# A convolution's taps move from VectorE to GpSimd, in a kernel of two chained MLPs

## The chip, the cores and the metric

One NeuronCore of a Trainium2 chip. The metric is the device time of one execution in microseconds, lower is better. Engines by the names of the profile: PE is TensorE's matmul, PEld its weight load, DVE is VectorE, ACT is ScalarE, POOL is GpSimd, SP is SyncE, which issues nearly all of the DMAs.

## The reference

A causal convolution over 7 positions whose taps are a softmax of `weight` (one set for each of 8 heads, 24 channels a head), and two MLPs behind it, all in float32. 8192 tokens (2 x 4096), 192 channels, hidden width 2048.

```python
w = exp(weight - max); w = w / (sum(w) + 1e-9)          # (8, 7)
out = einsum('hk,bskhg->bshg', w, x_unf)                # 7 taps for each channel
h = x @ w_in                                            # first MLP
g = where(h >= 1, h, where(h <= -1, 0, (h + 1)**2 / 4))
x = g @ w_out
h = x @ w_in2                                           # second MLP
g = h * (1 / (1 + exp(-1.702 * h)))
return g @ w_out2
```

## The kernel before

Tokens lie along the free dimension, channels on the partitions. The 8192 tokens are 16 blocks of T = 512. The 192 channels of a block are a tile of 128 (part 0, `xa`) and one of 64; the 64 last channels of two blocks that follow each other share one tile of 128 partitions (part 1, `xb`). So block pair j has three convolutions of seven taps over 128x512: part 0 of block 2j, the joint part 1, and part 0 of block 2j+1. A convolved tile is split into two float32r tiles, a high half copied by ACT and the rest subtracted by DVE (`split`, L72); the same is done with the hidden values and the weights, and a product is made of three such pairs.

The hidden width is cut into NF = 16 slices. A unit is one slice of one phase; a phase is one MLP of one block. The order of units is fixed (`units`, L219): blocks 0 and 1 of the first MLP in turn, four slices of each at a time (units 0 to 31), then block 2 (units 32 to 47), then the second MLP of blocks 0 and 1, and so on. One step of the first loop (L493, steps 0 to 47) makes `gemm1` of its unit (five matmuls into a PSUM bank `h`), its activation (`act_a`: ACT L272 and L273, DVE L274), the split of the unit before (`act_b`: ACT L73, DVE L74), `gemm2` of the unit four steps back (five matmuls into `acc`), and then what is planned beside it. From step 48 on two units go together (`both`).

What goes beside a step stands in `plan`: `at(step, op)` appends to a list, and `beside(step)` issues that list. The order within an engine is the order of issue; an engine waits only for data and buffers. Beside the first steps the weights are converted: `convert_at(1, f, ...)` loads slice f three steps ahead (`raw`, three buffers) and works on it in four steps, s to s+3, with s = f-2 for slices 4 to 7 and 2f-9 from slice 8 on: `begin` (ACT L117, DVE L118), `join` (DVE L122), `high_part` (ACT L127), `low_part` (DVE L131, L132). So the low part of slice 11 is issued at step 16 and wanted by unit 19, that of slice 15 at step 24 and wanted by unit 27.

The convolutions of blocks 0 and 1 are made ahead of the loop, on DVE and, with diagonal matrices `diag` (L165), on PE; POOL scales one set of these matrices (L167, seven multiplications of 128x128). All others are planned by `conv_at(j)`, L424, on DVE (`conv_taps`, L148: a multiplication L152, then six fused multiply-adds L153). For j = 1 the first unit of block 2 is 32 and that of block 3 is 80: its inputs are loaded at step 2, seven taps into `cva` stand at steps 10 to 16, `put_a` (the split) at 17, seven taps into `cvb` at 18 to 24, `put_b` at 25, and the taps of block 3's part 0 at 65 to 71.

The tag `o` (two buffers, pool `o_p`) holds the diagonals first and the outputs later. `xt` has two buffers for part 0 and one for part 1.

Of the kernel before, what the change touches and what calls it, by code (L numbers as in the profile page):

```python
# [8 lines left out]
F32 = mybir.dt.float32  # L9
# [6 lines left out]
P = 128  # L16
T = 512
# [3 lines left out]
def kernel(  # L21
# [21 lines left out]
    nc = tc.nc  # L43
    NBLK, D, _ = out.shape
    K = taps_in.shape[2]
    NF, _, WC = w1.shape
    DB = D - P
    B = P // DB
# [14 lines left out]
    o_p = ctx.enter_context(tc.tile_pool(name="o", bufs=2))  # L63
    ps = ctx.enter_context(tc.tile_pool(name="ps", bufs=1, space=bass.MemoryType.PSUM))

    def bank(n, name):
        return ps.tile([P, T], F32, tag=f"bank{n}", name=name)
# [4 lines left out]
    def split(src, hi, lo):  # L72
        nc.scalar.copy(hi, src)  # L73
        nc.vector.tensor_sub(lo, src, f32(hi))  # L74


    taps = const.tile([P, 2, K], F32, name="taps")
# [61 lines left out]
    def new_xs():  # L139
        return [xs_p.tile([P, T], F32R, tag=t, name=t) for t in ("xah", "xal", "xb", "xc")]  # L140

    def x_load(part, i):

        t = xt_p.tile([P, T + 64], F32, tag=f"xt{part}", name="xt", bufs=2 - part)[:, 0 : PAD + T]
        nc.sync.dma_start(t, (xb if part else xa)[i])
        return t

    def conv_taps(part, t, c):  # L148
        def tap(k):
            w, x = taps[:, part, k : k + 1], t[:, k : k + T]  # L150
            if k == 0:
                return lambda: nc.vector.tensor_scalar_mul(c, x, w)  # L152
            return lambda: nc.vector.scalar_tensor_tensor(c, x, w, c, op0=ALU.mult, op1=ALU.add)  # L153

        return [tap(k) for k in range(K)]

    def warm_up():

        w = bank(7, "warm")
        for _ in range(9):  # L160
            nc.tensor.matmul(w[:, 0:P], ident, ident, start=True, stop=True)
# [12 lines left out]
    def put_a(i, c):  # L174
        split(c, *x1[i][:2])

    def swap_halves(dst, src):
        nc.sync.dma_start(f32(dst[0:DB]), f32(src[DB:P]))
        nc.sync.dma_start(f32(dst[DB:P]), f32(src[0:DB]))

    def put_b(i, c):

        b, halved = i % B, phases.index((1, i)) * NF >= WHOLE
        t = x1[i][2 + (b if halved else 0)]
        hi, lo = (t[0:DB], t[DB:P]) if b == 0 else (t[DB:P], t[0:DB])
        split(c[b * DB : (b + 1) * DB], hi, lo)
        if halved:
            swap_halves(x1[i][3 - b], t)

    def conv_ops(j):  # L190

        ta, tb = xt[0, B * j], xt[1, j]
        ca = cv_p.tile([P, T], F32, tag="cva", name="cva")
        cb = cv_p.tile([P, T], F32, tag="cvb", name="cvb", bufs=1)
        x1[B * j] = new_xs()
        ops = conv_taps(0, ta, ca) + [lambda: put_a(B * j, ca)]
        ops += conv_taps(1, tb, cb) + [lambda: put_b(B * j, cb)]
        st = {}

        def begin():  # L200
            st["c"] = cv_p.tile([P, T], F32, tag="cva", name="cva")
            x1[B * j + 1] = new_xs()
            st["ops"] = conv_taps(0, xt[0, B * j + 1], st["c"])
            put_b(B * j + 1, cb)

        ops.append(begin)
        ops += [lambda: st["ops"].pop(0)() for _ in range(K)] + [lambda: put_a(B * j + 1, st["c"])]
        return ops
# [195 lines left out]
    def at(step, op):  # L404
        plan.setdefault(max(step, 0), []).append(op)
# [14 lines left out]
    def fetch_x(*which):  # L420
        for part, i in which:
            xt[part, i] = x_load(part, i)

    def conv_at(j):  # L424
        first, second = (unit_at[phases.index((1, B * j + k)), 0] for k in range(B))
        ops = []
        at(first - 30, lambda: fetch_x((0, B * j), (1, j), (0, B * j + 1)))
        at(first - 22, lambda: ops.extend(conv_ops(j)))
        for k in range(2 * (K + 1)):
            at(first - 22 + k, lambda: ops.pop(0)())  # L430
        for k in range(K + 2):
            at(second - 16 + k, lambda: ops.pop(0)())

    with tc.manual_schedule():
        nc.sync.dma_start(taps, taps_in)
# [5 lines left out]

        make_identity(nc, ident)
        warm_up()
        softmax_taps()

# [3 lines left out]
        ca = cv_p.tile([P, T], F32, tag="cva", name="cva")  # L449
# [31 lines left out]
        for j in range(1, NBLK // B):  # L481
            conv_at(j)
# [97 lines left out]
```

## Time and profile before

| | us |
|---|---|
| median of 3 runs | 1138.7 (1138.65 to 1138.96) |
| the profiled execution | 1138.51 |
| its span, first to last instruction | 1136.7 |
| PE busy | 1127.7 (99%) |
| ACT busy | 823.0 (72%) |
| DVE busy | 713.6 (63%) |
| POOL busy | 6.7 (1%, 13 instructions) |

A busy time is the sum over an engine's instructions; those of PE overlap, so a busy PE need not be PE at its peak. The shares are those of the whole span; the first 80 us have other shares than the rest. Times in rows count from the span's start. "idle before <- releaser" is the time in which an engine stood ahead of an instruction, and what ended that time.

### The profile page before, as it was taken

What the parts mean: (1) busy time and instruction counts of PE and PEld (TensorE: products, weight loads), DVE (VectorE), ACT (ScalarE), POOL (GpSimd) and SP (SyncE); (2) the same over time, 40 slices, a digit from 0 to 9 for tenths busy, and PEclk for the clock granted to TensorE, in tenths of its full rate; (3) what the DMA queues carried; (4) which work ended last, traced back from release to release, by engine and by line L of the source; (5) the groups of instructions that cost most, each with busy time, mean ns of one, the idle gap of its engine ahead of it and who ended that gap; (6) DMA issues with size and microseconds to landing.
All of it is one profiled execution on the core that took longest, in us unless ns stands there. A gap on an engine that the chain in (4) does not pass through costs nothing.

```text
span 1136.7 us, 22822 instructions
## 1 busy us (share of the span) xinstructions
PE 1127.7 (99%) x9324; PEld 927.1 (82%) x9324; DVE 713.6 (63%) x1152; ACT 823.0 (72%) x1468; POOL 6.7 (1%) x13
## 2 busy tenths in 40 slices
PE   9999999999999999999999999999999999999998
PEld 5878888888888888888888888888888888888886
DVE  7998765675557756476564756647566575655532
ACT  7989875867758677686776768677586776868654
POOL 2000000000000000000000000000000000000000
PEclk9999999999999999999999999999999999999999
DMA  5321420100001000010000100010000100000000
GB/s 176 124 65 43 123 76 11 57 10 25 10 11 43 17 18 10 11 43 20 15 19 12 33 20 15 20 43 1 20 15 20 44 1 20 15 20 15 11 15 14
DMA packets 16680, 36.40 MB, mean 32 GB/s; under 512 B 2497, under 2 KB 2753, under 8 KB 16577
## 3 DMA queue, kind: packets, MB, share of 16 engines
q1 hardware_dynamic: 16432, 34.82, 10.4%
q8 instruction: 73, 1.20, 0.5%
q14 instruction: 31, 0.25, 0.1%
q10 hardware_dynamic: 144, 0.13, 0.0%
HBM read 21.05 MB, written 6.29 MB: 24 GB/s over the span
## 4 chain that ended last, share of the span: by engine, by line
PE 94%; DVE 3%; ACT 2%; issue 1%; DMA 0%; SPq 0%
PE acc L361 46%; PE h L361 42%; PE acc L315 3%; PE h L250 3%; DVE glo L74 1%; DVE a L274 1%; PE ca_ps L170 1%; DVE wd L122 0%; DVE cva L153 0%; DMA raw<-in_w_dram 0%; ACT a L273 0%; ACT a L272 0%; ACT wa L117 0%; ACT wt L127 0%; DVE wt L131 0%
## 5 line engine op out<-in xcount | busy, mean ns | idle before, releaser
L361 PE MATMUL acc<-ghi,wt 64*128 64x512 f32 x2772 | 835.1, 386 | 0.0
L361 PE MATMUL h<-xah,wt 64*128 64x512 f32 x1848 | 713.6, 386 | 0.0
L361 PE MATMUL acc<-glo,wt 64*128 64x512 f32 x1848 | 678.0, 386 | 0.0
L361 PEld LDWEIGHTS acc<-ghi,wt 64*128 64x128 f32 x2772 | 468.5, 184 | 53.9 <-ACT ghi L73 0.3
L74 DVE TENSOR_TENSOR glo<-a,ghi 128x512 fp32r<-128x512 f32 x512 | 341.3, 688 | 232.9 <-ACT ghi L73 223.6
L361 PEld LDWEIGHTS acc<-glo,wt 64*128 64x128 f32 x1848 | 340.0, 184 | 36.5 <-DVE glo L74 0.8
L361 PEld LDWEIGHTS h<-xah,wt 64*128 64x128 f32 x1848 | 340.0, 184 | 36.2 <-issue 0.4
L361 PE MATMUL h<-xal,wt 64*128 64x512 f32 x924 | 356.8, 386 | 0.0
L73 ACT CAST ghi<-a 128x512 fp32r<-128x512 f32 x512 | 301.3, 614 | 26.2 <-DVE a L274 25.7
L274 DVE SCALAR_TENSOR_TENSOR a<-h,a 128x512 f32<-128x512 f32 x256 | 176.8, 690 | 159.7 <-ACT a L273 159.4
L276 ACT ACTIVATE a<-h 128x512 f32<-128x512 f32 x256 | 150.8, 596 | 153.9 <-PE h L361 146.0
L361 PE MATMUL h<-xb,wt 64*128 64x512 f32 x693 | 230.9, 386 | 0.0
L361 PE MATMUL h<-xc,wt 64*128 64x512 f32 x693 | 230.7, 386 | 0.0
L272 ACT ACTIVATE a<-h 128x512 f32<-128x512 f32 x256 | 151.0, 590 | 53.0 <-PE h L361 52.3
L361 PEld LDWEIGHTS h<-xal,wt 64*128 64x128 f32 x924 | 170.0, 184 | 17.9
L273 ACT ACTIVATE a<-a 128x512 f32<-128x512 f32 x256 | 161.8, 632 | 8.2
L361 PEld LDWEIGHTS h<-xc,wt 64*128 64x128 f32 x693 | 127.5, 184 | 17.9
L361 PEld LDWEIGHTS h<-xb,wt 64*128 64x128 f32 x693 | 127.4, 184 | 9.0
L153 DVE SCALAR_TENSOR_TENSOR cva<-xt,taps,cva 128x512 f32<-128x512 f32 x90 | 67.2, 747 | 1.3
L250 PE MATMUL h<-xah,wt 128*128 128x512 f32 x100 | 40.5, 405 | 2.6 <-DVE wt L131 2.6
L315 PE MATMUL acc<-ghi,wt 128*128 128x512 f32 x150 | 42.4, 390 | 0.0
L315 PEld LDWEIGHTS acc<-ghi,wt 128*128 128x128 f32 x150 | 28.1, 188 | 6.2 <-issue 0.4
(61 smaller groups left out, 455.3 us busy)
## 6 DMA issues: line engine op xcount, KB each, us to landing
raw<-in_w_dram SPq DMA_DIRECT2D x32, 448.0 KB, 3.4
xc<-xb SPq DMA_DIRECT2D x44, 128.0 KB, 2.2
xt<-in_xa_dram SPq DMA_DIRECT2D x16, 259.0 KB, 3.5
out_dram<-o SPq DMA_DIRECT2D x15, 256.0 KB, 2.0
out_dram<-o SPq DMA_DIRECT2D x17, 128.0 KB, 2.3
xt<-in_xb_dram SPq DMA_DIRECT2D x8, 259.0 KB, 3.2
xb<-xc SPq DMA_DIRECT2D x14, 128.0 KB, 2.2
out_dram<-o ACTq DMA_DIRECT2D x1, 128.0 KB, 1.8
```

The costliest lines, as they stand in the source:

```text
L73: nc.scalar.copy(hi, src)
L74: nc.vector.tensor_sub(lo, src, f32(hi))
L153: return lambda: nc.vector.scalar_tensor_tensor(c, x, w, c, op0=ALU.mult, op1=ALU.add)
L170: return lambda: nc.tensor.matmul(c, d[:, k], t[:, k : k + T], start=k == 0, stop=k == K - 1)
L250: nc.tensor.matmul(h, w, r, start=j == 0, stop=j == len(prods) - 1)
L272: nc.scalar.activation(a, h, AF.Relu, bias=0.5, scale=0.5)
L273: nc.scalar.activation(a, a, AF.Square)
L274: nc.vector.scalar_tensor_tensor(a, h, 1.0, a, op0=ALU.max, op1=ALU.min)
L276: nc.scalar.activation(a, h, AF.Gelu_apprx_sigmoid)
L315: nc.tensor.matmul(acc, w, r, start=id(acc) in fresh, stop=last and ends[id(acc)] == k)
L361: mm = nc.tensor.matmul(banks[n], w, r, start=n in fresh, stop=ends.get(n) == k)
```

## The change

For block pair 1 the fourteen taps of `cva` (block 2) and `cvb` (the joint 64 channels of blocks 2 and 3) are issued on POOL: the first tap of a set is a multiplication into the sum, each later one a multiplication into a tile `y` of tag `o` and an addition to the sum, 14 multiplications and 12 additions of 128x512. They are planned at steps 4 to 10 and 12 to 18; the splits `put_a` and `put_b` stay at 17 and 25, on ACT and DVE. Block 2's part 0 and the joint part 1 are loaded at step 1 instead of 2, block 3's part 0 at step 20 instead of 2. The taps of block 3's part 0 stay on DVE, at the steps where they were, and all other pairs stay as they are.

```diff
+    def conv_taps_aside(part, t, c, mul=nc.gpsimd.tensor_scalar_mul):
+        def tap(k):
+            w, x = taps[:, part, k : k + 1], t[:, k : k + T]
+
+            def op():
+                if k == 0:
+                    mul(c, x, w)
+                else:
+                    y = o_p.tile([P, T], F32, tag="o", name="y")
+                    mul(y, x, w)
+                    nc.gpsimd.tensor_add(c, c, y)
+
+            return op
+
+        return [tap(k) for k in range(K)]
...
-        ops = conv_taps(0, ta, ca) + [lambda: put_a(B * j, ca)]
-        ops += conv_taps(1, tb, cb) + [lambda: put_b(B * j, cb)]
+        conv = conv_taps_aside if j == 1 else conv_taps
+        ops = conv(0, ta, ca) + [lambda: put_a(B * j, ca)]
+        ops += conv(1, tb, cb) + [lambda: put_b(B * j, cb)]
...
-        at(first - 30, lambda: fetch_x((0, B * j), (1, j), (0, B * j + 1)))
-        at(first - 22, lambda: ops.extend(conv_ops(j)))
-        for k in range(2 * (K + 1)):
-            at(first - 22 + k, lambda: ops.pop(0)())
+        if j == 1:
+            steps = [*range(4, 4 + K), 17, *range(5 + K, 5 + 2 * K), 25]
+            at(1, lambda: fetch_x((0, B * j), (1, j)))
+            at(20, lambda: fetch_x((0, B * j + 1)))
+        else:
+            steps = range(first - 22, first - 22 + 2 * (K + 1))
+            at(first - 30, lambda: fetch_x((0, B * j), (1, j), (0, B * j + 1)))
+        at(steps[0], lambda: ops.extend(conv_ops(j)))
+        for k, step in enumerate(steps):
+            at(step, lambda k=k: ops[k]())
         for k in range(K + 2):
-            at(second - 16 + k, lambda: ops.pop(0)())
+            at(second - 16 + k, lambda k=k: ops[2 * (K + 1) + k]())
```

## Rows read from the trace of the kernel before

**Rows 1.** The page: PE's busy time, and its granted clock in 40 slices

```profile
PE 1127.7 (99%) x9324; PEld 927.1 (82%) x9324; DVE 713.6 (63%) x1152; ACT 823.0 (72%) x1468; POOL 6.7 (1%) x13
...
PEclk9999999999999999999999999999999999999999
```

**Rows 2.** Busy time by stretch: stretch, length, PE, PEld, DVE, ACT, POOL, clock, DMA, GB/s

```profile
22.50:44.00 21.50, 21.49 (x95) 17.47 (x94) 18.68 (x40) 20.83 (x39) 0.00 (x0) 1.00 0.50 167
44.00:58.90 14.90, 13.87 (x62) 11.15 (x61) 14.90 (x30) 13.04 (x25) 0.00 (x0) 1.00 0.30 85
58.90:79.10 20.20, 18.60 (x81) 14.88 (x81) 20.15 (x41) 17.41 (x32) 0.00 (x0) 1.00 0.23 75
79.10:130.00 50.90, 50.90 (x225) 42.14 (x225) 43.19 (x81) 47.82 (x88) 0.00 (x0) 1.00 0.25 75
```

**Rows 3.** Timeline of PE (start, us, instruction); last, a piece of the chain of waits

```profile
57.25 0.61 PE L315 MATMUL acc<-glo,wt 128*128 128x512 f32 x2
58.90 0.50 PE L250 MATMUL h<-xah,wt 128*128 128x512 f32 x1 [1.03 <-DVE wt L131]
...
79.08 0.50 PE L250 MATMUL h<-xah,wt 128*128 128x512 f32 x1 [1.60 <-DVE wt L131]
...
81.66 1.13 PE h L250 x5
```

**Rows 4.** Timeline of DVE, 44 to 51.3 us

```profile
44.20 0.48 DVE L152 TENSOR_SCALAR cva<-xt,taps 128x512 f32<-128x512 f32 x1
...
46.10 0.74 DVE L153 SCALAR_TENSOR_TENSOR cva<-xt,taps,cva 128x512 f32<-128x512 f32 x1
46.77 0.68 DVE L274 SCALAR_TENSOR_TENSOR a<-h,a 128x512 f32<-128x512 f32 x1
...
48.57 0.61 DVE L122 SCALAR_TENSOR_TENSOR wd<-wa,wd 128x448 uint32<-128x448 uint32 x1
49.11 0.74 DVE L153 SCALAR_TENSOR_TENSOR cva<-xt,taps,cva 128x512 f32<-128x512 f32 x1
...
50.97 0.38 DVE L118 TENSOR_SCALAR wd<-raw 128x448 uint32<-128x448 uint32 x1
51.28 0.73 DVE L153 SCALAR_TENSOR_TENSOR cva<-xt,taps,cva 128x512 f32<-128x512 f32 x1
```

**Rows 5.** Waits of DVE from 22.5 to 44 us: total, times, longest

```profile
DVE a L274 <- ACT a L273: 2.4, 4, 0.8
```

**Rows 6.** Timeline of SP's queue, 17 to 26 us; last, the page's DMA issues

```profile
17.93 0.33 SPq L98 DMA_DIRECT2D raw<-in_w_dram  x1
...
24.49 0.43 SPq L145 DMA_DIRECT2D xt<-in_xa_dram  x1
...
xt<-in_xa_dram SPq DMA_DIRECT2D x16, 259.0 KB, 3.5
```

**Rows 7.** Timeline of ACT: the first halves of the splits of `cva` and `cvb`

```profile
60.54 0.60 ACT L73 CAST xah<-cva 128x512 fp32r<-128x512 f32 x1
...
79.86 0.62 ACT L73 CAST xb<-cvb 64x512 fp32r<-64x512 f32 x1 [1.09 <-DVE cvb L153]
```

**Rows 8.** POOL's groups by line and shape: count, busy us, mean ns, idle before

```profile
masks.py:199 POOL TENSOR_SCALAR_AFFINE_SELECT ident<-ident 128x128 f32<-128x128 f32 x1 | 0.3, 294 | 0.1
masks.py:197 POOL MEMSET ident<- 128x128 f32 x1 | 0.2, 205 | 0.3 <-POOLq L566 0.3
...
L566 POOL MEMSET const-float32-0.0<- 128x1 f32 x1 | 0.1, 99 | 0.2 <-issue 0.2
```

**Rows 9.** `diag` and L153 (ns min/median/max, first and last start); timelines of POOL and DVE

```profile
L167 POOL TENSOR_SCALAR diag<-ident,taps x7: 794/807/1260, 4.2 to 9.4; 128x128 f32<-128x128 f32 x7
...
L153 DVE SCALAR_TENSOR_TENSOR cva<-xt,taps,cva x90: 733/747/779, 4.6 to 1010.8; 128x512 f32<-128x512 f32 x90
...
5.82 0.81 POOL L167 TENSOR_SCALAR diag<-ident,taps 128x128 f32<-128x128 f32 x1
...
5.41 0.75 DVE L153 SCALAR_TENSOR_TENSOR cva<-xt,taps,cva 128x512 f32<-128x512 f32 x1
```

## The prediction

> **What bounds the kernel now.** I read the page first: TensorE (PE) is busy in 99% of the span and its granted clock stands at the upper of its two levels (2.4 GHz) in all 40 slices [rows 1]. So only time in which PE stands still can be won, and the table of stretches says where that is [rows 2]: nothing to speak of from 22.5 to 44 us, 1.0 us from 44 to 58.9, 1.6 us from 58.9 to 79.1, and nothing from there to 130 us. TensorE's timeline names one cause for both, VectorE's `wt` of L131, the low half of a converted weight slice: 1.03 us ahead of 58.90 and 1.60 ahead of 79.08 [rows 3]. Matmul starts give the size. Normal ones follow each other at 0.23 (1.13 for five); the last pair ahead of the first stall starts at 57.25, so its second near 57.48, and the next starts 1.42 later at 58.90. Less 0.23 that is 1.2 lost, and by the same surplus over the wait the second stall is 1.8: 3.0 us together [rows 3]. **3.0 us is all that can be won** (0.26%), and it is won only if neither stall is left.
>
> Why is `wt` late? From 44 to 79 us VectorE (DVE) has practically no idle time (14.90 of 14.90 us busy, then 20.15 of 20.20, [rows 2]), and two steps of it take 5.17 us (46.10 to 51.28, from one tap to the tap two steps later, [rows 4]), 2.58 a step, where PE needs 2 x 1.13 = 2.27 for one (five matmuls of `h`, five of `acc`, [rows 3]). So DVE falls behind by 0.31 a step, and PE pays for it when it comes to slices 11 and 15. Before that, from 22.5 to 44, ScalarE is the tight one (20.83 of 21.50 us busy, [rows 2]), and DVE is idle for 21.50 - 18.68 = 2.8 us [rows 2], 2.4 of them waiting for ScalarE [rows 5].
>
> **What is taken away.** Fourteen DVE taps of steps 10 to 25. In the packed stream a later tap moves the next operation by 0.66 (46.10 to 46.77, so 0.08 less than it lasts), the first by some 0.40 (0.48 less 0.08) [rows 4]. Seven are 0.40 + 6 x 0.66 = 4.4 us, both sets 8.8. Without them two steps cost 5.17 - 2 x 0.66 = 3.84, that is 1.92 a step, under PE's 2.27: DVE would then catch up, and with nothing against it both stalls go.
>
> **What moves beside it.** The loads of block 2's `xt` and of the joint `xt` go from step 2 to step 1, on SP's queue ahead of slice 7's load instead of behind it. Slice 6, of step 1, was issued at 17.93, and the first `xt` load at 24.49, right behind slice 7, which had waited for its buffer [rows 6]. So they leave at about 18.4 and 18.9, land some 3.5 us later (the page's median for this load, [rows 6]), near 22 us, in a stretch in which the queue was empty, and delay nobody; slice 7 should even land earlier. Block 3's `xt` goes to step 20 and is wanted at step 64. All of this I cost at nothing; its cover is the empty queue from 18.3 to 24, and without it slice 7 would be late by the two loads' issue, 2 x 0.43 us.
>
> **What GpSimd (POOL) has to do.** 14 multiplications and 12 additions of 128x512, each waiting for the one before; they start as soon as `xt` is there, near 22 us, whatever step they are written at, since nothing else is in POOL's queue. The new waits are ScalarE's: `xah<-cva` (60.54 before) and `xb<-cvb` (79.86 before) now wait for POOL, and behind them on ScalarE stand the activations of the next step [rows 7]. The trace of before has no such POOL operation. The nearest rows [rows 8]: a fill of 128 columns takes 205 ns and one of 1 column about 100, so 0.83 ns a column; a one-input pass over 128 columns 294 ns, so about 1.5 ns a column. By these a 512-column multiplication streams for 0.43 to 0.78 us, and an addition, which reads twice as much, for 0.86 to 1.56. I take 0.5 and 1.1, near the low ends, for a reason that follows. The seven `diag` multiplications of the prologue, only 128 columns each, took 0.79 to 1.26 us, most of them 0.81 [rows 9]; times four, with some long ones among them, 3.5 us would be the far end.
>
> **What it costs DVE.** This decides the case. The `diag` rows beside DVE's [rows 9] show POOL waiting for DVE. All seven end 0.4 to 0.5 us behind the end of the DVE operation that they met, whatever their own start: the one of 5.82 ends at 6.63, 0.47 behind the tap that ended at 5.41 + 0.75 = 6.16; one missed a gap and lasted 1.26. So POOL gets in only where DVE leaves off. The other way, four of the six taps beside it took 0.75, as undisturbed ones do, and two took 0.78; 779 ns is the largest of all 90 on the line, whose median is 747: 128 columns cost DVE at most 0.03 us, because they fit into the pause between two operations of DVE. From that I read that POOL keeps DVE out for roughly its streaming time (0.1 us for 128 columns), less some 0.1 of pause. 512 columns don't fit: 0.5 - 0.1 = 0.4 us for a multiplication and 1.1 - 0.1 = 1.0 for an addition, when the next DVE operation reads SBUF twice.
>
> Not every one does. `a` of L274 (0.68 less 0.08, so 0.60 of each step, [rows 4]) reads PSUM and one SBUF tile, and I assume that it runs beside POOL. Of the 3.84 us of two steps, 1.2 are such an `a` (31%); 0.84 are the `wd` operations before an `a` (48.57 to 49.11 and 50.97 to 51.28, [rows 4]; 22%); 47% are neither. POOL that gets ready in the last collides in full; ready within an `a`, it has 0.3 free on average; ready before an `a`, 0.6. A multiplication then costs DVE 0.47 x 0.4 + 0.31 x 0.1 = 0.22, an addition 0.47 x 1.0 + 0.31 x 0.7 + 0.22 x 0.4 = 0.78; together 14 x 0.22 + 12 x 0.78 = **12.4 us**, more than the 8.8 taken away. By the low streaming ends it is 14 x 0.16 + 12 x 0.54 = 8.8, by the high ones 14 x 0.46 + 12 x 1.24 = 21.2.
>
> When does it fall? An operation of POOL takes half a DVE operation of waiting (0.3), 0.35 of its own around the stream, and the stream: 1.15 and 1.75. That is 37 us in all, from 22 to 59: `cva` at about 41 (wanted at 60.5), `cvb` at 59 (wanted at 79.9), so ScalarE's new waits cost nothing, with 20 us to spare each. But nearly all of POOL's work lies ahead of the first stall, and only half of the taps do.
>
> **The sum.** Up to 58.9: DVE +12.4 from POOL, -4.4 for seven taps, -2.8 that its idle time before 44 takes up = +5.2 us. PE had lost 1.2 by then, so 6.4 now. (Part of it will show earlier, as waits for slices 4 to 10 between 30 and 58.) Behind 59 us DVE needs 1.92 a step, under PE's 2.27, and the second stall goes. So PE loses 6.4 instead of 3.0: **+3.4 us**. The profiled execution took 1138.5 (span 1136.7 and 1.8 around it), which is 0.2 under the median of the runs, 1138.7; so 1141.9, told as **1142.0**. By the ends: streams at the low rates, 8.8 - 2.8 - 4.4 + 1.2 - 3.0 = -0.2, 1138.3; at the high ones POOL works until about 68, taps of 6.1 us fall away by then, DVE's own lag adds 1.2: 21.2 - 2.8 - 6.1 + 1.2 + 1.2 - 3.0 = +11.7, 1150. If DVE's idle time takes up nothing because ScalarE is pushed along with it, 2.8 more than the forecast, 1144.8.
>
> The Trainium skill (GPSIMD Engine Reference, section 3.1) gives 4497 ns for an addition over 2048 float32 columns, so some 1.1 us for 512 as an estimate; with that as the addition's stream the sum is the forecast's, and no run so far shows it.
>
> **The rivals.** *DVE isn't held up* (faster). If POOL waits for DVE, as the `diag` rows show, but hardly the reverse, as the taps at 0.75 show, DVE is relieved of 4.4 us ahead of each stall and both go: -3.0, **1135.5**. ScalarE doesn't step in: its own work from 44 to 79 is below PE's, 13.04 of 14.90 and 17.41 of 20.20 us with the stalls in it [rows 2]. This needs POOL's whole cost to DVE up to 59 us under about 6 us, half of my estimate. For it: no row shows DVE held for more than 0.03. Against it: no row shows a POOL operation that is longer than DVE's pause.
>
> *A near draw* (no change): POOL streams at the rate of the fill and DVE loses about what it is relieved of, 8.8 against 8.8; 1137 to 1140, worked out above as 1138.3.
>
> *POOL holds DVE for its whole operation*, not for its stream alone. Then a multiplication keeps DVE out for 0.35 + 0.5 = 0.85 and an addition for 1.45: DVE loses 0.47 x 0.75 + 0.31 x 0.45 + 0.22 x 0.15 = 0.53 and 0.47 x 1.35 + 0.31 x 1.05 + 0.22 x 0.75 = 1.13 for one, 21 us in all, +12.0 by the same sum, **1150.5**. Against it: the `diag` operations, with 0.45 us behind the gap, would have put 0.3 on every tap that they met, and put 0.03 on two. The Trainium skill states this rule (SBUF — State Buffer, section "Who interferes with whom"): VectorE with two SBUF inputs and a GpSimd operation that reads SBUF share one pair of ports, which goes to whichever starts first for its whole instruction, while the other is blocked. The trace agrees on POOL's side (1.26 us for 128 columns) and not, or not for so long, on DVE's.
>
> *POOL is late*: at the far end of 3.5 us an operation, `cva` comes at 22 + 13 x 3.5 = 68, 7 us late, and `cvb` at 113, 33 us late; ScalarE stands at `xah` and `xb` with the activations behind, and the time is over 1160. At half of that both are in time.
>
> **How the numbers follow.** Forecast (a lock of about the stream, 1139.5 to 1146.5): 0.44. DVE hardly held up, 1135.3 to 1136.5: 0.29. Near draw: 0.17. Whole-instruction lock, 1146.5 to 1152: 0.07. POOL late: 0.03. A measurement here tells some 0.2% (2.3 us) from no change. Faster by more than that means under 1136.4: 0.30. Slower means over 1141.0: most of the forecast's case and the last two, 0.46. Between: 0.24. Both signs hold much, so the forecast's own range is 1139.5 to 1146.5; the range for 8 in 10 reaches from the floor of 1135.3 to 1147.0, and leaves out what is above.
>
> **What the profile after will show.** DVE's 128x512 operations from 22 to 60 us: if many `glo` and `wd` last 1 us or more instead of 0.6 to 0.7, DVE is held out by POOL; if all keep their length, the first rival is right. POOL's 26 operations should end near 59, the additions about 0.6 us longer than the multiplications. PE's waits for `wt` should come between 30 and 59 with some 6 us in sum, and none from 60 to 80; with the first rival none at all. ScalarE should not wait for `cva` or `cvb`. A stall of PE behind 80 us would make the working wrong altogether.

## The result, and the profile after

| | us |
|---|---|
| before, median of 4 runs | 1138.7 |
| after, median of 4 runs | 1148.7 (1148.5 to 1149.4) |
| ratio, 95% interval | 1.0086 (1.0074 to 1.0098) |
| predicted | 1142.0 (1135.3 to 1147.0) |

The change makes the kernel slower by 10.0 us. The side was forecast, the size was not: 3.4 us were, and the time lies above the range.

The page of the changed kernel: its span, the busy times, and the granted clock in 40 slices.

```profile
span 1147.6 us, 22846 instructions
...
PE 1133.0 (99%) x9324; PEld 928.1 (81%) x9324; DVE 718.9 (63%) x1138; ACT 823.7 (72%) x1468; POOL 49.4 (4%) x39
...
PEclk9999999999999999999999999999999999999999
```

Fourteen instructions of DVE are gone (x1152 to x1138, beside [rows 1]), and yet DVE is busy for 718.9 us instead of 713.6. That is the first hint: what is left takes longer. The groups of DVE by shape from 22 to 67 us of the changed kernel, and below them POOL's groups (count, busy us, mean ns, idle before), say which:

```profile
L74 DVE TENSOR_TENSOR glo<-a,ghi 128x512 fp32r<-128x512 f32 x13 | 12.2, 942 | 0.0
L291 DVE SCALAR_TENSOR_TENSOR a<-h,a 128x512 f32<-128x512 f32 x14 | 9.5, 682 | 2.9 <-ACT a L290 2.9
L122 DVE SCALAR_TENSOR_TENSOR wd<-wa,wd 128x448 uint32<-128x448 uint32 x8 | 6.9, 857 | 0.0
L131 DVE TENSOR_TENSOR wt<-wd,wt 128x384 fp32r<-128x384 f32 x7 | 6.4, 917 | 0.0
L118 DVE TENSOR_SCALAR wd<-raw 128x448 uint32<-128x448 uint32 x8 | 5.9, 732 | 0.0
L132 DVE TENSOR_TENSOR wt<-wd,wt 128x64 fp32r<-128x64 f32 x7 | 4.1, 584 | 0.0
...
L166 POOL TENSOR_SCALAR y<-xt,taps 128x512 f32<-128x512 f32 x12 | 22.7, 1895 | 0.0
L167 POOL TENSOR_TENSOR cva<-cva,y 128x512 f32<-128x512 f32 x6 | 8.2, 1364 | 0.5
L167 POOL TENSOR_TENSOR cvb<-cvb,y 128x512 f32<-128x512 f32 x6 | 7.9, 1321 | 0.5
```

The same stretch of the kernel before:

```profile
L274 DVE SCALAR_TENSOR_TENSOR a<-h,a 128x512 f32<-128x512 f32 x18 | 12.3, 684 | 2.7 <-ACT a L273 2.6
L74 DVE TENSOR_TENSOR glo<-a,ghi 128x512 fp32r<-128x512 f32 x18 | 12.2, 678 | 0.0
L122 DVE SCALAR_TENSOR_TENSOR wd<-wa,wd 128x448 uint32<-128x448 uint32 x10 | 6.2, 616 | 0.0
L131 DVE TENSOR_TENSOR wt<-wd,wt 128x384 fp32r<-128x384 f32 x9 | 4.9, 549 | 0.0
...
L118 DVE TENSOR_SCALAR wd<-raw 128x448 uint32<-128x448 uint32 x11 | 4.2, 383 | 0.0
L132 DVE TENSOR_TENSOR wt<-wd,wt 128x64 fp32r<-128x64 f32 x9 | 1.9, 216 | 0.0
```

`a` (L274 before, L291 here) keeps its length, 682 ns for 684. Everything that reads SBUF alone is longer: `glo` 942 ns for 678, L122 857 for 616, L131 917 for 549, L132 584 for 216, L118 732 for 383. Times their counts that is 13 x 0.26 + 8 x 0.24 + 7 x 0.37 + 7 x 0.37 + 8 x 0.35 = **13.3 us** by which POOL prolongs DVE's work. One operation beside another shows how; first DVE's timeline, then POOL's, of the changed kernel:

```profile
29.35 1.50 DVE L118 TENSOR_SCALAR wd<-raw 128x448 uint32<-128x448 uint32 x1
...
35.59 1.31 DVE L132 TENSOR_TENSOR wt<-wd,wt 128x64 fp32r<-128x64 f32 x1
...
38.69 0.68 DVE L74 TENSOR_TENSOR glo<-a,ghi 128x512 fp32r<-128x512 f32 x1
39.28 1.61 DVE L131 TENSOR_TENSOR wt<-wd,wt 128x384 fp32r<-128x384 f32 x1
...
40.96 1.02 DVE L122 SCALAR_TENSOR_TENSOR wd<-wa,wd 128x448 uint32<-128x448 uint32 x1
41.91 0.68 DVE L291 SCALAR_TENSOR_TENSOR a<-h,a 128x512 f32<-128x512 f32 x1
42.51 1.80 DVE L74 TENSOR_TENSOR glo<-a,ghi 128x512 fp32r<-128x512 f32 x1
...
29.31 1.29 POOL L167 TENSOR_TENSOR cva<-cva,y 128x512 f32<-128x512 f32 x1
...
38.88 1.61 POOL L167 TENSOR_TENSOR cva<-cva,y 128x512 f32<-128x512 f32 x1
40.47 1.92 POOL L166 TENSOR_SCALAR y<-xt,taps 128x512 f32<-128x512 f32 x1
42.47 1.29 POOL L167 TENSOR_TENSOR cva<-cva,y 128x512 f32<-128x512 f32 x1
```

An addition adds 1.1 us to the DVE operation that meets it (L131 1.61 for 0.55, `glo` 1.80 for 0.68), a multiplication 0.4 (L122 1.02 for 0.62). L118, which reads a single SBUF tile, is held no less than the others (1.50 for 0.38, beside an addition). The profile books this as busy time of DVE, not as a wait.

Where PE pays: the changed kernel's waits of PE from 25 to 200 us (total, times, longest), and two of the matmuls behind them.

```profile
PE h L267 <- DVE wt L131: 5.9, 5, 2.7
PE acc L332 <- DVE glo L74: 1.4, 3, 0.9
...
40.95 0.50 PE L267 MATMUL h<-xah,wt 128*128 128x512 f32 x1 [2.68 <-DVE wt L131]
...
71.03 0.50 PE L267 MATMUL h<-xah,wt 128*128 128x512 f32 x1 [2.12 <-DVE wt L131]
```

Against [rows 3], the matmul of slice 11 starts at 71.03 instead of 58.90, and the wait of 1.60 for slice 15 has become 0.49. A new stall stands at 40.95, ahead of every tap that the change takes from DVE (the first stood at 44.20, [rows 4]). That is where the account of the prediction broke, and a table of stretches makes it exact. DVE's `a` of unit n is the (n+1)th of its line, so its starts mark off equal work: units 3, 8 and 19 start it at 24.89, 37.12 and 65.08 us before, and at 27.30, 45.55 and 76.81 after. The rows are the stretch, its length, the busy time of PE, PEld, DVE, ACT and POOL, then the granted clock, the DMA share and GB/s, of the kernel before:

```profile
24.89:37.12 12.23, 12.23 (x56) 10.12 (x55) 11.44 (x24) 12.07 (x24) 0.00 (x0) 1.00 0.66 218
37.12:65.08 27.96, 26.93 (x119) 22.00 (x118) 27.11 (x55) 24.66 (x46) 0.00 (x0) 1.00 0.32 99
65.08:90.92 25.84, 24.24 (x107) 19.53 (x106) 23.09 (x43) 22.43 (x42) 0.00 (x0) 1.00 0.12 36
```

and of the changed one:

```profile
27.30:45.55 18.25, 15.00 (x58) 11.13 (x57) 18.25 (x25) 13.61 (x26) 17.83 (x12) 0.91 0.32 102
45.55:76.81 31.26, 27.65 (x115) 20.76 (x114) 28.87 (x47) 23.24 (x43) 20.39 (x13) 1.00 0.31 97
76.81:101.80 24.99, 24.50 (x108) 19.96 (x108) 19.38 (x37) 22.72 (x42) 0.00 (x0) 1.00 0.11 38
```

- Units 3 to 8: 12.23 to 18.25, **+6.0**. DVE's busy time rises by 6.8, its idle time falls from 0.8 to nothing. No tap stood here.
- Units 8 to 19: 27.96 to 31.26, **+3.3**. DVE is prolonged by about 6.2, eight taps fewer give back 4.8 by the prediction's prices (busy 27.11 to 28.87), and DVE's idle time *grows*, from 0.85 to 2.39.
- Units 19 to 31: 25.84 before, 24.99 after, -0.9: the second stall, of which 0.5 is left.
- Ahead of unit 3: 27.30 - 24.89, +2.4, in the profiled execution (it took 1149.4; the other three, which were not traced, took 1148.5 to 1148.8). POOL's new work starts at 22.93, and PE is 2.4 late by 21.15 already; see the last section.

Together 2.4 + 6.0 + 3.3 - 0.9 = 10.8, and the span is longer by 10.9. From unit 3 to its end the profiled execution takes 1147.6 - 27.30 = 1120.3 us, and 1136.7 - 24.89 = 1111.8 before: 8.5 of the loss lie there, and this is the part that the experiments below explain. What makes up the rest of the 10.0 between the medians is not shown.

### The profile page after: what moved, and what is told of

It reads as the page before. It is cut to its first block, busy times and chain, and to the rows that moved or that the text cites. A ratio compares the mean times of both kernels' runs of the same rounds, so it can differ in the third digit from the quotient of the medians.

```text
span 1147.6 us, 22846 instructions
## 1 busy us (share of the span) xinstructions
PE 1133.0 (99%) x9324; PEld 928.1 (81%) x9324; DVE 718.9 (63%) x1138; ACT 823.7 (72%) x1468; POOL 49.4 (4%) x39
## 4 chain that ended last, share of the span: by engine, by line
PE 93%; DVE 4%; ACT 1%; issue 1%; DMA 0%; SPq 0%; DVEq 0%
PE acc L378 46%; PE h L378 41%; PE acc L332 3%; PE h L267 3%; DVE glo L74 1%; DVE wd L122 1%; PE ca_ps L186 1%; DVE wt L131 0%; DMA raw<-in_w_dram 0%; ACT a L290 0%; DVE wd L118 0%; ACT a L289 0%; ACT wt L127 0%; DVE a L291 0%; ACT wa L117 0%
## 5 line engine op out<-in xcount | busy, mean ns | idle before, releaser
L378 PE MATMUL h<-xah,wt 64*128 64x512 f32 x1848 | 713.6, 386 | 0.0
L74 DVE TENSOR_TENSOR glo<-a,ghi 128x512 fp32r<-128x512 f32 x512 | 344.8, 695 | 232.8 <-ACT ghi L73 223.6
L291 DVE SCALAR_TENSOR_TENSOR a<-h,a 128x512 f32<-128x512 f32 x256 | 176.8, 690 | 164.4 <-ACT a L290 164.2
L153 DVE SCALAR_TENSOR_TENSOR cva<-xt,taps,cva 128x512 f32<-128x512 f32 x84 | 62.8, 747 | 1.3
L127 ACT CAST wt<-wd 128x448 fp32r<-128x448 f32 x32 | 18.1, 566 | 24.9 <-DVE wd L122 24.9
```

The costliest lines, as they stand in the source:

```text
L127: nc.scalar.copy(w[:, 0:WC], f32(st["d"]))
L291: nc.vector.scalar_tensor_tensor(a, h, 1.0, a, op0=ALU.max, op1=ALU.min)
L378: mm = nc.tensor.matmul(banks[n], w, r, start=n in fresh, stop=ends.get(n) == k)
```

## The experiments

The theory: POOL keeps DVE out of SBUF while it reads, and PE pays for it nearly in full. Rivals: the moved loads, ScalarE waiting for POOL's results, the mere number of POOL's instructions.

**The moved loads alone.** The kernel before with the loads of the change.

```diff
-        at(first - 30, lambda: fetch_x((0, B * j), (1, j), (0, B * j + 1)))
+        if j == 1:
+            at(1, lambda: fetch_x((0, B * j), (1, j)))
+            at(20, lambda: fetch_x((0, B * j + 1)))
+        else:
+            at(first - 30, lambda: fetch_x((0, B * j), (1, j), (0, B * j + 1)))
```

> The kernel before with only the loads moved as in the change: block 2's and the joint xt at step 1, block 3's at step 20; the taps stay on DVE at their old steps. If the moved loads cost nothing: within 0.5 us of the kernel before, 1138.2 to 1139.2. If the 2.4 us that PE loses ahead of 25 us in the trace of the changed kernel come from these loads: about 1141.

1139.0 us, ratio 1.0002 (0.9993 to 1.0011). The loads cost nothing.

**POOL's work beside the old taps.** DVE keeps all its taps; POOL multiplies and adds into tiles that nobody reads. The loads are those of the change. Pieces of the edit against the kernel before:

```diff
+    def conv_taps_aside(part, t, mul=nc.gpsimd.tensor_scalar_mul):
...
+                y = o_p.tile([P, T], F32, tag="o", name="y")
+                mul(y, x, w)
+                if k > 0:
+                    nc.gpsimd.tensor_add(y, y, x)
...
+        if j == 1:
+            aside.extend(conv_taps_aside(0, ta) + conv_taps_aside(1, tb))
...
+        if j == 1:
+            for k in range(2 * K):
+                at(4 + k, lambda k=k: aside[k]())
```

> The fourteen DVE taps as before, and beside them POOL's 14 multiplications and 12 additions into tiles that nobody reads (so its work is done twice and no engine waits for POOL). If the loss is DVE being held out of SBUF by POOL: slower than the changed kernel by at least the 8.8 us of taps that DVE keeps, so 1156 to 1162. If it is ScalarE waiting for POOL's results or anything else in the new order: within 1 us of the kernel before.

1150.1 us, ratio 1.0101 (1.0084 to 1.0118). No engine waits for POOL here, and the loss is there, so the wait for POOL's results and the new order are out. But it is only 1.4 us more than the change, where I had expected at least 8.8 more. From unit 3 on (1148.4 - 25.06 = 1123.3) it is 3.0 more. Either way the fourteen taps were worth little to begin with.

**The relief alone.** The changed kernel with no convolution on POOL, and twelve of the fourteen taps left out.

```diff
+    def conv_first(part, t, c):
+        return conv_taps(part, t, c)[:1] + [lambda: None] * (K - 1)
...
-        conv = conv_taps_aside if j == 1 else conv_taps
+        conv = conv_first if j == 1 else conv_taps
```

> The changed kernel without POOL's convolution: DVE makes the first tap of each of the two sets, at steps 4 and 12, and the other twelve taps are left out, so block 2 and the joint channels are wrong. What the relief of DVE is worth by itself. By the prediction's floor both stalls of PE go and the time is 1135.5 to 1136.0. If the order of the steps or the loads cost something by themselves: 1138 or more.

1136.7 us, ratio 0.9983 (0.9973 to 0.9992): 2.0 us and not 3.0. A wait of 0.5 us for slice 15 is left. The stretch of units 8 to 19 in this run, columns as above:

```profile
39.55:66.06 26.51, 26.51 (x117) 21.68 (x116) 23.09 (x47) 24.38 (x45) 0.00 (x0) 1.00 0.37 114
```

PE is busy for all of it and DVE idle for 3.4 us: with DVE out of the way the stretch can't be shorter than 26.51. Taking 4.0 us of work from DVE there (27.11 to 23.09) wins 27.96 - 26.51 = **1.45 us**, as long as PE is the one that has no room.

**Multiplications alone, additions alone.** Both are the changed kernel with part of POOL's work. The first leaves the additions out:

```diff
                     mul(y, x, w)
-                    nc.gpsimd.tensor_add(c, c, y)
```

The second adds shifted inputs without products:

```diff
-                    y = o_p.tile([P, T], F32, tag="o", name="y")
-                    mul(y, x, w)
-                    nc.gpsimd.tensor_add(c, c, y)
+                    nc.gpsimd.tensor_add(c, c, x)
```

> The changed kernel with POOL's twelve additions left out (the products stay in y; the sums of block 2 and the joint channels are the first tap only). In the trace of the changed kernel a multiplication prolongs the DVE operation that it meets by 0.3 to 0.4 us, an addition by 1.1. If the additions carry the loss: 14 x 0.4 = 5.6 us at the most against 8.8 us of relief, so both stalls nearly gone, 1135.5 to 1138. If the number of POOL's instructions or its clock-independent overhead carries it: half of the loss stays, 1142 or more.

> The changed kernel with POOL's twelve products left out and the additions made on shifted inputs (block 2 and the joint channels get an unweighted sum): 2 multiplications and 12 additions. The twelve multiplications alone with two first taps cost 2.3 us over the relief (1138.97 against 1136.69). In the changed kernel's trace an addition prolongs the DVE operation that it meets by 1.1 us, a multiplication by 0.4. If that direct price decides, the additions cost 12 x 1.1 = 13 us less what meets no such operation, so 1143 to 1147. If the price goes by the number of POOL's instructions, about as with the multiplications: 1139.

1139.0 (ratio 1.0005, 0.9996 to 1.0015) and 1143.9 (1.0041, 1.0026 to 1.0056). Over the relief alone that is 2.3 us for fourteen multiplications, and 7.2 for twelve additions with two multiplications; both together cost 12.0 in the changed kernel. From unit 3 on, in the profiled executions, it is 2.4, 7.7 and 10.8. Each of the two runs has fourteen instructions on POOL, so the price doesn't go by their number; the additions, which read two tiles, carry most of it. The first came out above what I expected of it.

**POOL that only writes.** The kernel before with 52 fills of 128x512.

```diff
+    def fill():
+        for _ in range(4):
+            nc.gpsimd.memset(o_p.tile([P, T], F32, tag="o", name="y"), 0.0)
...
+            for k in range(13):
+                at(3 + k, fill)
```

> The kernel before, and beside it 52 fills of 128x512 on POOL into tiles that nobody reads, from about 22 us on: POOL writes and reads nothing. If only POOL's reads hold DVE out: within 0.5 us of the kernel before. If its writes do too, at 0.4 us of each fill: 52 x 0.4 = 21 us of DVE, so 1148 or more. If only the operations of DVE that read one SBUF tile (L118, L152) are held by writes: 1139 to 1143.

1139.5 us, ratio 1.0027 (1.0003 to 1.0051). Three of the ten executions took 1146.5 to 1149.3 us, at a mean granted clock of 0.995 or 0.996 where the others had 1.00; they were not traced, and why they were longer is open. The profiled execution took 1139.1. POOL's group and three of DVE's from 22 to 52 us in it:

```profile
L426 POOL MEMSET y<- 128x512 f32 x36 | 18.3, 557 | 0.2
...
L74 DVE TENSOR_TENSOR glo<-a,ghi 128x512 fp32r<-128x512 f32 x12 | 8.2, 681 | 0.0
...
L118 DVE TENSOR_SCALAR wd<-raw 128x448 uint32<-128x448 uint32 x8 | 3.9, 488 | 0.0
L131 DVE TENSOR_TENSOR wt<-wd,wt 128x384 fp32r<-128x384 f32 x6 | 3.3, 550 | 0.0
```

18 us of fills (36 of the 52) leave `glo` (681) and L131 (550) as they were; only L118, with one input, is longer, 488 for 383. So, as far as the profiled execution shows, what holds DVE's two-input operations out is POOL's *reading*. The Trainium skill (SBUF — State Buffer, section "Who interferes with whom") says just that: VectorE with two SBUF inputs contends with a GpSimd instruction that reads SBUF and not with one that only writes. The two traces agree. The same page of the Trainium skill (section "SBUF: two separate sides") also says that the loser is blocked for the whole instruction, and there the measurement decides otherwise: the multiplications lasted 1.9 us on average (POOL's own wait included) and cost DVE 0.4.

**Half of the work on POOL.** The changed kernel with block 2's taps on POOL and the joint ones back on DVE.

```diff
-        ops += conv(1, tb, cb) + [lambda: put_b(B * j, cb)]
+        ops += conv_taps(1, tb, cb) + [lambda: put_b(B * j, cb)]
...
-            steps = [*range(4, 4 + K), 17, *range(5 + K, 5 + 2 * K), 25]
+            steps = [*range(4, 4 + K), 17, *range(18, 18 + K), 25]
```

> The changed kernel with only block 2's 13 operations on POOL (from 23 to about 44 us); the joint taps go back to DVE at steps 18 to 24. If the prediction's account holds, in which seven taps of relief and DVE's idle time are set against POOL's price up to the first stall: 7.1 - 4.4 - 2.8 leaves nothing, the first stall stays at 1.2 and the second at 1.8 or less, 1138 to 1138.7. If what PE loses by step 8, where no tap was taken away yet, is not given back (6.0 us in the changed kernel), and the seven taps behind it are worth 1.4 as in the run without taps: 6.0 - 1.4 = 4.6 us, 1143 to 1143.5.

1144.4 us, ratio 1.0046 (1.0031 to 1.0062). Its units 3 to 8 and 8 to 19, columns as above:

```profile
24.74:42.69 17.95, 13.88 (x59) 10.57 (x58) 17.95 (x24) 13.63 (x26) 17.53 (x11) 1.00 0.33 104
42.69:70.69 28.00, 26.48 (x116) 21.25 (x115) 24.16 (x48) 23.56 (x44) 2.33 (x2) 1.00 0.34 108
```

The first stretch loses 5.7 us with half of the operations, and it is not given back: the second, in which DVE has seven taps fewer and is busy for 24.16 of 28.00 us, takes as long as before (27.96), although POOL is nearly done by then. The prediction's account would have put this run at no change. The granted clock is 1.00 in both stretches, so the lower clock of the changed kernel in its first one (0.91) is not what makes the 6.0 us there.

**The same work later.** The changed kernel with POOL's start moved from 22.93 to 36.67 us.

```diff
-            steps = [*range(4, 4 + K), 17, *range(5 + K, 5 + 2 * K), 25]
-            at(1, lambda: fetch_x((0, B * j), (1, j)))
-            at(20, lambda: fetch_x((0, B * j + 1)))
+            steps = [*range(9, 9 + K), 22, *range(10 + K, 10 + 2 * K), 29]
+            at(8, lambda: fetch_x((0, B * j), (1, j)))
+            at(26, lambda: fetch_x((0, B * j + 1)))
```

> The changed kernel with POOL's work some 20 us later: loads at step 8, taps from step 9, the splits at 22 and 29, so that POOL works from about 42 to 86 us, behind the stretch in which ScalarE is nearly full. If POOL's price to DVE (13 us) counts in full wherever it falls, since nothing of it is taken up by idle time: again 1147 to 1150. If the early place is the matter (ScalarE and DVE are both full from 22 to 44 us and wait for each other in turn), DVE without taps has 2.27 - 1.92 = 0.35 us of room a step behind that, some 6 us over the 18 steps: 1140 to 1144.

1145.3 us, ratio 1.0052 (1.0037 to 1.0067), between the two expectations: 8.6 us over the relief alone instead of 12.0. From unit 3 on the two profiled executions differ by 2.0 (1143.0 - 24.71 = 1118.3). So the early place costs some, but the later one that was tried has no room for this load either.

**The taps where DVE has room.** The prediction's own reading ([rows 2 to 4]) says that DVE is over-full only because a tap stands beside every step. So: the kernel before, nothing on POOL, block 2's taps at odd steps, the joint ones at 25 to 28.

```diff
...
+        steps = range(first - 22, first - 22 + 2 * (K + 1))
+        if j == 1:
+            steps = [11, 13, 15, 17, 19, 21, 23, 24, 25, 25, 26, 26, 27, 27, 28, 29]
...
```

> The kernel before with nothing on POOL, but block 2's and the joint taps moved on DVE to where it has room: block 2's at the odd steps 11 to 23, beside which no weight slice is finished, its split at step 24, and the joint ones at 25 to 28, its split at 29. If DVE's load ahead of slices 11 and 15 makes the two stalls: four and seven taps fewer ahead of them, 2.6 and 4.7 us, so both are gone but for the 0.66 that is left in the run without the taps: 1136.5 to 1137.0. If the later splits come too late for unit 32: 1139 or more, with a new wait of PE near 91 us.

1138.0 us, ratio 0.9993 (0.9983 to 1.0002), not to be told from no change. Both stalls are gone: PE comes from unit 3 to unit 27 in 54.19 us instead of 56.94 (from the start of the second matmul, `h<-xal`, of the one to that of the other). But PE, now ahead, waits elsewhere; this run's timeline of PE:

```profile
112.74 0.73 PE L315 MATMUL acc<-glo,wt 128*128 128x512 f32 x2 [0.33 <-DVE glo L74]
...
131.58 0.49 PE L361 MATMUL acc<-glo,wt 64*128 64x512 f32 x1 [0.64 <-DVE glo L74]
```

That is where the second MLP's weights are converted beside the splits of blocks 0 and 1. Moving these too, alone and with the taps:

```diff
-            s = 2 * NF - 1 + 9 * f // 4
+            s = 2 * NF + 4 + 2 * f
```

> The kernel before with only the later conversion of the second MLP's weights (from step 36, one every two steps). If the two stalls at 58.9 and 79.1 us are what the moved taps win, they stay here and the time is that of the kernel before, 1138.3 to 1139.0. If the later conversion is what e9_odd_w2 won by: 1135.2 to 1136.

> The run with the taps at DVE's free steps (e6_odd, 1138.04), and the second MLP's weight slices converted from step 36 on, one every two steps, instead of from 31 on, one every 2.25. In e6_odd PE lost 0.5 and 0.8 us at 112.7 and 131.6 us, where these conversions meet the splits of blocks 0 and 1; with them later these stalls should go: 1136.5 to 1137.5, the two stalls of the kernel before gone. If the conversions are then late for unit 48 and after: a wait of PE for wt behind 130 us and no gain.

Alone 1137.5 us, ratio 0.9990 (0.9981 to 0.9999); with the taps **1135.2 us, ratio 0.9965 (0.9952 to 0.9977)**, faster than both kernels. PE's row for the stretch of the second stall, alone and with the taps (columns as above):

```profile
58.90:79.10 20.20, 18.59 (x80) 14.86 (x80) 20.15 (x40) 17.41 (x32) 0.00 (x0) 1.00 0.08 29
```

```profile
58.90:79.10 20.20, 20.20 (x89) 16.38 (x88) 19.75 (x40) 18.86 (x35) 0.00 (x0) 1.00 0.08 23
```

With the taps moved PE has no wait left from 25 to 200 us. The 1.2 us that the later weights win by themselves I had not expected: both stalls stand as before in that run. Most of it lies between 140 and 160 us, where PE gets through 180 matmuls instead of 172, first before and then with the later weights (columns as above):

```profile
140.00:160.00 20.00, 20.00 (x172) 17.03 (x170) 11.68 (x26) 13.67 (x27) 0.00 (x0) 1.00 0.28 84
```

```profile
140.00:160.00 20.00, 20.00 (x180) 16.52 (x178) 14.55 (x32) 15.98 (x31) 0.00 (x0) 1.00 0.43 130
```

PE counts as busy throughout in both, and the trace names no wait of PE that went; why it was slower there stays open.

## Why the prediction was right or wrong, point by point

- **What bounds the kernel, and the two stalls** [rows 2, 3]: right. Moving fourteen taps to where DVE has room takes both away, and with the later weights 2.3 us more than these alone (1137.5 to 1135.2). The floor of 3.0 us was a little too deep: the two stalls are worth 2.75 (54.19 for 56.94). With the taps left out the second stall keeps 0.5 of waiting, and 2.0 are won.
- **The loads**: right, no cost.
- **POOL's pace and ScalarE's new waits**: nearly right. POOL ended at 66 us instead of 59, since a multiplication took 1.9 us and not 1.15 (how much of that is waiting for a gap isn't shown), and an addition 1.34 and not 1.75; the additions are thus the shorter ones, not the longer as foreseen. ScalarE waited for neither `cva` nor `cvb`.
- **What POOL costs DVE**: right, as a mechanism and in size. Additions 1.1 for the 1.0 foreseen, multiplications 0.4 for 0.4, `a` untouched, 13.3 us in all for 12.4. Only the condition "reads SBUF twice" was too narrow: 2.8 of the 13.3 us are L118's, which reads one tile. The rival without hold-up falls, and so does the one with the whole instruction.
- **The sum: wrong, and this is the step that failed**: "Up to 58.9: DVE +12.4 from POOL, -4.4 for seven taps, -2.8 that its idle time before 44 takes up". It is one account for 36 us, and the work has due dates within them. In the changed kernel the term that broke is the last one: DVE's idle time took up nothing and grew (next point), which is 3.5 of the 4.1 us that units 3 to 19 lost beyond the forecast. The account also passes over the order of things: by unit 8 6.0 us were lost, ahead of the first tap, while PE waited for slices 4 to 7, and what DVE gains afterwards can't buy that back. The prediction even said in brackets that part of it would show earlier, and didn't draw the consequence. The run with half of the work on POOL shows it for the -4.4 too: it lost 5.7 us in that stretch, and the seven taps behind it didn't return them; DVE's time went into idling instead (28.00 - 24.16 = 3.8 us).
- **The idle time** that should have taken up 2.8 us: the stretch of units 3 to 19 had 1.65 of it, and ended with 2.39. DVE's idle time there is waiting for ScalarE (2.2 of the 2.39 for `a`), and ScalarE, in order, waits for DVE's `wd`, from 22 to 80 us for 4.2 us before and 11.9 after:

```profile
ACT wt L127 <- DVE wd L122: 4.2, 8, 0.8
```

```profile
ACT wt L127 <- DVE wd L122: 11.9, 8, 2.3
```

I read this as a hold of 1.1 us that passes through both and comes back as idle time; no run takes the loop apart. 2.8 + 0.7 = 3.5 us of the error are here. The prediction had named the case that "ScalarE is pushed along with it", at 1144.8, and didn't choose it.

- **The sizes, for units 3 to 19**: 5.2 foreseen, +0.9 for POOL's price, +3.5 for the idle time, -0.4 for the eighth tap in the stretch: 9.2; measured 6.0 + 3.3 = 9.3. Behind it -0.9 instead of -1.8, since 0.5 of the second stall is left. With the 2.4 ahead of unit 3, for which the prediction had no term, this is all of the difference in the profiled execution; of the 10.0 between the medians about 1.5 stay without an explanation. (Two slips of the working, 8.8 for 14 x 0.16 + 12 x 0.54 = 8.7 and 5.17 for 51.28 - 46.10 = 5.18, move nothing.)
- **What the profile was to show**: partly right. `glo`, L131 and L122 do last 1.0 to 1.8 us where POOL meets them. But PE waited for `wt` for 3.2 us up to 59 us, not some 6, then for 2.1 at 71.03, where none was foreseen, and for 0.5 at 89.96. This last one is what is left of the second stall, some 11 us later than before; it lies behind the 80 us that the prediction had made the sign of a working that is wrong altogether.

## What to carry to other kernels

Work that is moved to GpSimd beside a full VectorE isn't free for VectorE: an addition from SBUF cost it 1.1 us here, more than the fused tap of 0.75 that it replaced. Draw the account for each due date, not for a stretch: relief that comes behind a stall doesn't pay for what was lost ahead of it, and idle time in a loop of two engines that wait for each other takes nothing up. Where an engine is over-full for 30 us and has room in the next 10, moving its own operations in time was cheaper here than moving them to another engine.

## What the runs showed of the hardware that was not expected

The time that an engine is held out stands in the length of its instruction: L132, 64 columns, lasted 1.31 us at 35.59 for its 0.22, and no row calls it a wait. Busy shares hide such a loss, means by shape show it.

The start differs between executions. In the profiled one of the changed kernel DVE's first operation on a weight slice started at 7.32 us (6.66 before), PE stood still longer ahead of 14 us, and the granted clock was 0.60 from 14 to 18.3 us, so partly at the lower level (1.2 GHz), where it was 1.00 before. PE's second matmul of unit 0 was 0.8 us late (12.89 for 12.12), that of unit 2 was 2.4 late (21.15 for 18.74). The profiled execution of the run without the taps had the same start (unit 3 at 27.32) and took 1138.6, the others of that run 1136.1 to 1136.9. A later first slice does not always come with the lower clock: in the profiled executions of the multiplications alone and the additions alone it was worked on from 7.81 and 7.61, and the clock was 1.00.

Whether this start belongs to the change is open. The run with half of the work, the same program up to step 11, had a clock of 1.00 there and unit 3 at 24.74. But the three other executions of the changed kernel, with the same mean clock of 0.997 as the profiled one, were only 0.6 to 0.9 us faster than it, and none of them was traced. Later, behind the stall at 40.95, the clock was 0.69 from 41 to 44 us; the run with half of the work lost 5.7 us over the same units at 1.00.
